# Scaling attention scores in place in PSUM, with their extreme kept as the exponential's bias

## The chip, the core and the metric

The kernel runs on one core of one Trainium2 chip. The metric is the device time of one execution in microseconds (us); lower is better.

## What is computed

A clustered attention feeds two dense layers. There are 2 batches, 8 heads, 768 positions and a head width of 64. A query sees only the keys that have the same nearest centroid (16 centroids per head); where no key has it, every score is the same constant and the softmax is uniform.

```
mask = q_assign[:, :, :, None] == k_assign[:, :, None, :]
scores = scale * np.matmul(q, k.transpose(0, 1, 3, 2))
scores = np.where(mask, scores, -1000000000.0)
scores = scores - np.max(scores, axis=-1, keepdims=True)
attn = np.exp(scores)
attn = attn / (np.sum(attn, axis=-1, keepdims=True) + 1e-09)
x = attn @ v            # then 1536 tokens x 512
h = x @ w_in;  x = (h * sigmoid(h)) @ w_out         # layer 1, 512 -> 2048 -> 512
h = x @ w2_in; y = (max(h,0) + alpha*min(h,0)) @ w2_out   # layer 2, same sizes
```

## The kernel before, in words

**Number format.** All matrix products run on pairs of 16-bit parts (a high and a low half). Before a tensor is split it is brought into range by a power of two (`pow2_scale`, L158); the inverse factors are kept in small columns: `isk` for the keys of a head pair, `q_inv` for the queries of a tile.

**Units.** Attention is cut into 96 units: 12 query tiles of 128 queries (6 for each batch) times 8 heads. Unit u is tile `n = u // 8`, head `h = u % 8`; heads go in 4 pairs that share the prepared keys and values. The function `front` (L449) makes one unit's probabilities:

- TensorE forms 128x768 scores in a two-bank PSUM tile `s` (there are two such tiles), as two halves of 384 columns. For each half one matmul over 80 rows (L459) and one over 128 rows (L463) accumulate. Rows 64 to 79 of the 80-row operands hold the cluster code: the query side is 0 at its own cluster and 2^15 elsewhere, the key side is -2^15 at its own cluster and 0 elsewhere, so that a pair in different clusters gets -2^30.
- VectorE reduces the 768 scores of each query to the negated maximum (L475), then makes in two operations on one column the scale (L478: the product of the inverse factors, or 0 where the maximum shows that no key was in the query's cluster) and the bias (L479: maximum times scale).
- ScalarE computes `exp(scale * score + bias)` from PSUM into SBUF with the row sum as a second output (L481), and copies the result to 16 bits (L488). VectorE subtracts to get the low half (L490). Both go into one of two `hl` buffers.
- A DMA transposes the 128x1536 16-bit block (L496, issued from SyncE's queue, SP). Nothing else issues DMAs, so loads of weights, keys and values stand in that queue too.

`back(u - 2)` multiplies the transposed probabilities of the unit two before by the values (L508, 18 matmuls of 64 columns). After a tile's eighth head `x_done` (L521) normalizes the tile and hands it to layer 1.

**Preparation of keys and queries.** `prep_k_b` (L380) forms the similarities of keys and centroids in the one-bank PSUM tile `m` (one buffer), `one_hot` (L271, L277 to L285) turns them into the cluster code on VectorE, and a DMA transposes the code. It runs once for each of 2 batches and 4 pairs: in batch 0 ahead of unit 0 and after units 0, 2 and 4, in batch 1 after units 44, 46, 48 and 50. `prep_q_b` (L426) does the same for the queries of the next tile, at head 4 of each tile. Sums over partitions (`all_sum`, L207) use the same `m` tile.

**Order of work.** The program text interleaves units with 16 + 16 steps of layer 1 for each of 7 chunks of query tiles (17 units go first; after the chunks 32, 53, 64, 69 and then all 96 units have been issued), and with tasks that convert the weights of layer 1. After the last unit the weights of layer 2 are converted in the background, and layer 2 follows. A planner that runs when the kernel is built then lays out each engine's queue from that text: by priority, and by when its own timing says that operands are ready. On the chip each queue is in order, so an instruction that waits holds back all that stand behind it on that engine.

```
nc.vector.tensor_reduce(out=nm, in_=sc[:, :, :hs], axis=AX.XY, op=ALU.max, negate=True)
nc.vector.tensor_scalar(scl, nm, 2.0 ** 29, d[:, pr:pr + 1], op0=ALU.is_lt, op1=ALU.mult)
nc.vector.tensor_scalar(bias, nm, scl, None, op0=ALU.mult)
```

Of the kernel before, what the change touches and what calls it, by code (L numbers as in the profile page):

```python
# [9 lines left out]
F32 = mybir.dt.float32  # L10
# [36 lines left out]
def cluster_attention_silu_prelu(  # L47
# [44 lines left out]
    def view(off, dt, *dims):  # L92
        n = 1
        for d in dims:
            n *= d
        nb = n * (2 if dt in (F16, BF16) else 4)
        assert off % 4 == 0 and nb % 4 == 0 and off + nb <= total, (off, nb)
        a = arena[:, off // 4:(off + nb) // 4]
        if dt != F32:
            a = a.bitcast(dt)  # L100
        if len(dims) == 1:
            return a
        names = [f"a{i}" for i in range(len(dims))]
        pat = f"p ({' '.join(names)}) -> p {' '.join(names)}"
        return a.rearrange(pat, **{n: d for n, d in zip(names, dims)})
# [39 lines left out]
    def col(n):  # L145
        a = stat[:, nstat[0]:nstat[0] + n]
        nstat[0] += n
        assert nstat[0] <= NSTAT
        return a
# [25 lines left out]
    def scr(n):  # L175
        if scr_pos[0] + n > NSCR:
            scr_pos[0] = 0
        a = scr_cols[:, scr_pos[0]:scr_pos[0] + n]
        scr_pos[0] += n
        return a  # L180
# [55 lines left out]


    half = small_p.tile([128, 12], F32, name="half")

    def prep_centroids():  # L240
        craw = view(o_xf, F32, D)
        nc.sync.dma_start(out=craw, in_=centroids.rearrange("h c d -> (h c) d"))
        nc.vector.memset(ones, 1.0)
        nc.vector.memset(half, 0.5)
        nc.scalar.activation(out=scr(1), in_=half[:, 0:1], func=ACTF.Sqrt)
        make_identity(nc, ident)
        for c in range(C):
            nc.gpsimd.memset(rev[:, c:c + 1], float(C - c))
# [22 lines left out]
    def one_hot(sims, n, w2, o, a, b):  # L271


        y = view(o + KB, F16, n, C)
        z = view(o, F16, n, C)
        m = scr(n)
        nc.vector.reduce_max(out=m, in_=sims, axis=AX.X)  # L277
        nc.vector.tensor_tensor(out=y, in0=sims, in1=bc(m, C), op=ALU.is_equal)
        nc.vector.tensor_tensor(
            out=z, in0=y, in1=rev.unsqueeze(1).to_broadcast([128, n, C]), op=ALU.mult  # L280
        )
        m2 = scr(n // 2).bitcast(F16)
        nc.vector.reduce_max(out=m2, in_=z, axis=AX.X)
        nc.vector.tensor_tensor(out=y, in0=z, in1=bc(m2, C), op=ALU.is_equal)
        nc.vector.tensor_scalar(w2[:, :, D:D + C], y, a, b, op0=ALU.mult, op1=ALU.add)  # L285
# [9 lines left out]
    def k_pre(b, pr):  # L295
        return o_x2 + 6 * KB * pr if b == 0 else o_x2 + (8 + 6 * (pr % 2)) * KB
# [83 lines left out]
    def prep_k_b(b, pr):  # L380
        did.add(("k", b, pr))
        kt1 = view(o_kt1 + 3 * KB * pr, F16, G, 128)
        w2 = view(k_pre(b, pr) + 3 * KB, F16, G, 128)
        sims = psum("m", G, C)
        for g in range(G):
            h = 2 * pr + g // T
            for i, c in enumerate((0, 2)):
                nc.tensor.matmul(
                    out=sims[:, g], lhsT=kt1[:, g], rhs=cw[:, c, h * C:(h + 1) * C],
                    start=(i == 0), stop=(i == 1),  # L390
                )
        one_hot(sims, G, w2, k_pre(b, pr), -MASK, 0.0)
        k_t2[b, pr] = nc.sync.dma_start_transpose(
            out=view(o_kt2 + 3 * KB * pr, F16, G, 128), in_=w2.rearrange("p a b -> p (a b)")
        )


# [28 lines left out]
    def prep_q_b(n):  # L426
        qt1 = view(o_qt + 4 * KB * (n % 2), F16, H, 128)
        w2 = view(o_preq + 2 * KB, F16, H, 128)
        sims = psum("m", H, C)
        for h in range(H):  # L430
            for i in range(2):
                nc.tensor.matmul(
                    out=sims[:, h], lhsT=qt1[:, h], rhs=cw[:, i, h * C:(h + 1) * C],
                    start=(i == 0), stop=(i == 1),
                )
        one_hot(sims, H, w2, o_preq, -MASK, MASK)
        q_t2[n] = nc.sync.dma_start_transpose(
            out=view(o_qt + 4 * KB * (n % 2) + 2 * KB, F16, H, 128),
            in_=w2.rearrange("p a b -> p (a b)"),
        )  # L440


    q_inv = col(2)
    sums = [col(H) for _ in range(2)]
    un_cols = col(24)
    pt_of = {}
    x_ps = {}

    def front(u):  # L449
        n, h = divmod(u, H)  # L450
        b, pr = n // T, h // 2
        sc = ps_s.tile([128, 2, 512], F32, tag="s", name="s")
        qt1 = view(o_qt + 4 * KB * (n % 2), F16, H, 128)
        qt2 = view(o_qt + 4 * KB * (n % 2) + 2 * KB, F16, H, 128)
        kt1 = view(o_kt1 + 3 * KB * pr, F16, 2, T * 128)
        kt2 = view(o_kt2 + 3 * KB * pr, F16, 2, T * 128)
        hs = S // 2
        for j in range(2):
            nc.tensor.matmul(  # L459
                out=sc[:, j, :hs], lhsT=qt2[0:D + C, h],  # L460
                rhs=kt2[0:D + C, h % 2, j * hs:(j + 1) * hs], start=True, stop=False,
            )
            nc.tensor.matmul(  # L463
                out=sc[:, j, :hs], lhsT=qt1[:, h],
                rhs=kt1[:, h % 2, j * hs:(j + 1) * hs], start=False, stop=True,
            )
        d = un_cols[:, 12 + NP * (n % 2):12 + NP * (n % 2) + NP]
        if h == 0:
            nc.vector.tensor_scalar(
                d, isk[b], q_inv[:, n % 2:n % 2 + 1], 1.0 / float(D) ** 0.5,  # L470
                op0=ALU.mult, op1=ALU.mult,
            )
        c0 = 4 * (u % 3)
        nm, scl, bias = (un_cols[:, c0 + i:c0 + i + 1] for i in range(3))
        nc.vector.tensor_reduce(  # L475
            out=nm, in_=sc[:, :, :hs], axis=AX.XY, op=ALU.max, negate=True
        )
        nc.vector.tensor_scalar(scl, nm, 2.0 ** 29, d[:, pr:pr + 1], op0=ALU.is_lt, op1=ALU.mult)  # L478
        nc.vector.tensor_scalar(bias, nm, scl, None, op0=ALU.mult)  # L479
        o = p_buf()  # L480
        nc.scalar.activation(  # L481
            out=view(o, F32, 2, hs), in_=sc[:, :, :hs], func=ACTF.Exp, scale=scl, bias=bias,
            accum_out=sums[n % 2][:, h:h + 1],
        )
        p = view(o, F32, S)
        i = u % 2
        hl = view(o_hl + 3 * KB * i, F16, 2, S)
        nc.scalar.activation(out=hl[:, 0], in_=p, func=ACTF.Copy)  # L488
        en = nc.vector if u in P_LO_DVE else nc.gpsimd
        en.tensor_tensor(out=hl[:, 1], in0=p, in1=hl[:, 0], op=ALU.subtract)  # L490
        pt = view(o_pt + 3 * KB * (u % NPT), F16, 2 * T, 128)
        pt_of[u] = pt
# [584 lines left out]
```

## Time and profile before

| what | value |
|---|---|
| device time, median of 3 runs | 875.75 us (872.88, 875.75, 876.51) |
| profiled execution, first to last instruction (span) | 873.1 us; no device time of its own is given for it |
| busy share of the span: TensorE matmuls / weight loads | 83% / 58% |
| VectorE (DVE) / ScalarE (ACT) / GpSimd (POOL) | 69% / 53% / 13% |
| DMA, mean share of 16 engines | 54.2% |

PE is TensorE's matmuls and PEld its weight loads, which overlap. A row of a group of instructions gives its source line, engine, operation, what it writes and reads, the count, busy us and mean ns of one, and the idle time of the engine just before. A row of waits gives who waited for whom, the total us, how often, and the longest. In the rows of order in time the first two numbers are start and length in us. The span is 2.65 us below the median of the runs.

### The profile page before, as it was taken

The numbers are of one execution on the slowest core, as the hardware profiler recorded it, in microseconds if no ns is written. First come the engines' busy times: TensorE is split into PE (matmuls) and PEld (weight loads), VectorE is DVE, ScalarE is ACT, GpSimd is POOL, SyncE is SP. The second block draws the span as 40 slices with busy tenths as digits, with TensorE's granted clock in tenths as the row PEclk, the third lists the DMA queues.
The fourth block names the chain that finished last, engine by engine and source line by source line (L and its number), as shares of the span: only waits on it lengthen the run. The fifth ranks groups of instructions, "written<-read, shape, count | busy, mean of one in ns | idle before, by whom it ended". The sixth has DMA issues, their size and how long they took to land.

```text
span 873.1 us, 16736 instructions
## 1 busy us (share of the span) xinstructions
PE 721.3 (83%) x6740; PEld 503.3 (58%) x6740; DVE 598.1 (69%) x1366; ACT 459.6 (53%) x825; POOL 109.8 (13%) x89
## 2 busy tenths in 40 slices
PE   2456457668688888899799996899898999999998
PEld 1344346566576776688677786787443444444443
DVE  6899988898978957855975884677995058206700
ACT  7945666747857745745754764868561014102200
POOL 3512200070202210000000001012046000000000
PEclk9965558969999999999999999899998999999999
DMA  9998996767897794763785696227300000000000
GB/s 281 246 258 205 264 205 134 116 121 147 161 171 119 139 164 73 146 116 46 126 121 100 112 212 153 97 98 252 135 1 1 37 12 1 13 25 12 1 25 25
DMA packets 241598, 101.89 MB, mean 117 GB/s; under 512 B 217329, under 2 KB 227569, under 8 KB 241393
## 3 DMA queue, kind: packets, MB, share of 16 engines
q1 hardware_dynamic: 241520, 100.83, 54.2%
q8 instruction: 53, 0.87, 0.4%
q14 instruction: 25, 0.20, 0.1%
HBM read 44.08 MB, written 3.15 MB: 54 GB/s over the span
## 4 chain that ended last, share of the span: by engine, by line
PE 41%; DMA 12%; DVE 9%; ACT 3%; issue 2%; POOL 0%; SPq 0%; POOLq 0%; ACTq 0%; DVEq 0%
PE w L979 10%; DMA arena<-arena 9%; PE w L948 7%; PE w L876 6%; PE m L979 5%; PE w L845 5%; PE m L948 3%; PE x L508 2%; DMA arena<-in_moe_w_in_dram 1%; DMA arena<-in_moe_w_out_dram 1%; DVE stat L475 1%; DVE arena L595 1%; PE s L463 1%; PE s L459 1%; DVE arena L856 1%
## 5 line engine op out<-in xcount | busy, mean ns | idle before, releaser
L845 PE MATMUL w<-arena 128*128 128x256 f16 (+1 forms) x1212 | 132.1, 263 | 14.7 <-DVE arena L852 7.3
L845 PEld LDWEIGHTS <-arena 128*128 128x128 f16 x1344 | 119.3, 101 | 36.3 <-issue 12.9
L508 PE MATMUL x<-arena 128*128 128x64 f16 x1728 | 74.1, 201 | 74.8 <-DMA arena<-arena 74.8
L876 PEld LDWEIGHTS <-arena 128*128 128x128 f16 x1344 | 119.4, 101 | 21.0 <-POOL arena L606 4.0
L876 PE MATMUL w<-arena 128*128 128x256 f16 (+1 forms) x1200 | 124.4, 262 | 6.3 <-POOL arena L606 3.7
L508 PEld LDWEIGHTS <-arena 128*128 128x128 f16 x1728 | 65.2, 103 | 88.7 <-DMA arena<-arena 87.0
L481 ACT ACTIVATE arena<-s,stat 128x768 f32<-128x768 f32 x96 | 94.4, 984 | 41.3 <-DVE stat L479 35.6
L490 DVE TENSOR_TENSOR arena<-arena 128x768 f16<-128x768 f32 x96 | 93.3, 973 | 28.6 <-ACT arena L488 28.1
L475 DVE TENSOR_REDUCE stat<-s 128x1 f32<-128x768 f32 x96 | 91.2, 952 | 29.1 <-PE s L463 28.7
L979 PEld LDWEIGHTS <-arena 128*128 128x128 f16 x576 | 56.8, 99 | 71.8 <-issue 5.1
L948 PEld LDWEIGHTS <-arena 128*128 128x128 f16 x576 | 56.6, 99 | 71.5 <-issue 6.8
L488 ACT ACTIVATE arena<-arena 128x768 f16<-128x768 f32 x96 | 80.5, 840 | 28.3 <-DMA arena<-arena 27.7
L979 PE MATMUL w<-arena 128*128 128x512 f16 x384 | 85.4, 383 | 2.4 <-DVE arena L958 2.4
L948 PE MATMUL w<-arena 128*128 128x512 f16 x384 | 86.4, 379 | 0.8 <-DVE arena L958 0.8
L594 POOL TENSOR_SCALAR arena<-arena,stat 128x1024 f16<-128x1024 f32 x20 | 33.8, 1696 | 401.3 <-DVE stat L168 269.3
L961 ACT ACTIVATE arena<-arena,stat 128x512 f16<-128x512 f32 x48 | 34.3, 720 | 88.5 <-DVE arena L958 88.5
L459 PE MATMUL s<-arena 80*128 80x384 f16 x192 | 69.6, 362 | 5.3 <-DMA arena<-arena 2.7
L463 PE MATMUL s<-arena 128*128 128x384 f16 x192 | 69.9, 364 | 0.0
L573 ACT ACTIVATE arena<-arena 128x1024 int32<-128x1024 uint32 x32 | 36.6, 1145 | 47.9 <-DMA arena<-in_moe_w_in_dram 32.4
L851 ACT ACTIVATE arena<-w,stat 128x256 f32<-128x256 f32 (+1 forms) x101 | 43.8, 434 | 29.2 <-PE w L845 25.4
L957 DVE TENSOR_SCALAR arena<-w,stat 128x512 f32<-128x512 f32 x32 | 23.9, 748 | 46.8 <-PE w L948 46.6
L584 DVE SCALAR_TENSOR_TENSOR arena<-arena 128x1024 int32<-128x1024 int32 x32 | 39.1, 1222 | 24.4 <-ACT arena L577 24.4
(141 smaller groups left out, 1035.4 us busy)
## 6 DMA issues: line engine op xcount, KB each, us to landing
arena<-in_moe_w_in_dram SPq DMA_DIRECT2D x16, 1024.0 KB, 6.0
arena<-in_moe_w_out_dram SPq DMA_DIRECT2D x16, 1024.0 KB, 5.0
arena<-in_k_dram SPq DMA_DIRECT2D x8, 384.0 KB, 4.1
arena<-in_q_dram SPq DMA_DIRECT2D x6, 512.0 KB, 4.5
arena<-in_v_dram SPq DMA_DIRECT2D x8, 384.0 KB, 6.2
out_dram<-arena SPq DMA_DIRECT2D x12, 256.0 KB, 2.0
arena<-arena SPq DMA_TRANSPOSE x149, 4.1
arena<-in_moe_alpha_dram SPq DMA_DIRECT2D x1, 1024.0 KB, 5.1
```

The costliest lines, as they stand in the source:

```text
L459: nc.tensor.matmul(out=sc[:, j, :hs], lhsT=qt2[0:D + C, h], rhs=kt2[0:D + C, h % 2, j * hs:(j + 1) * hs], start=True, stop=False,)
L463: nc.tensor.matmul(out=sc[:, j, :hs], lhsT=qt1[:, h], rhs=kt1[:, h % 2, j * hs:(j + 1) * hs], start=False, stop=True,)
L475: nc.vector.tensor_reduce(out=nm, in_=sc[:, :, :hs], axis=AX.XY, op=ALU.max, negate=True)
L481: nc.scalar.activation(out=view(o, F32, 2, hs), in_=sc[:, :, :hs], func=ACTF.Exp, scale=scl, bias=bias, accum_out=sums[n % 2][:, h:h + 1],)
L488: nc.scalar.activation(out=hl[:, 0], in_=p, func=ACTF.Copy)
L490: en.tensor_tensor(out=hl[:, 1], in0=p, in1=hl[:, 0], op=ALU.subtract)
L508: nc.tensor.matmul(out=x_ps[0][:, h], lhsT=pt[:, ph * T + t], rhs=vt[:, h % 2, t, vh], start=(i == 0), stop=(i == 3 * T - 1),)
L845: nc.tensor.matmul(out=hp, lhsT=wi[:, a, kd, f % 2 * 128:f % 2 * 128 + 128], rhs=mov(bb, kd), start=(i == 0), stop=(i == 3 * KD - 1),)
L851: nc.scalar.activation(out=th, in_=hp, func=ACTF.Tanh, scale=dh[:, f // 2:f // 2 + 1])
L876: nc.tensor.matmul(out=acc, lhsT=wo[:, a, f % 2, dt * 128:(dt + 1) * 128], rhs=g[:, f, bb], start=(i == 0), stop=(i == 3 * KF - 1),)
L948: nc.tensor.matmul(out=hp, lhsT=in_piece(o_a + 24 * KB, f // 2)[:, a, kd, f % 2 * 128:][:, :128], rhs=x[bb][:, kd], start=(i == 0), stop=( ...
L979: nc.tensor.matmul(out=acc, lhsT=g[:, f, a, t * 128:(t + 1) * 128], rhs=out_piece(o_w, f // 2)[:, bb, f % 2], start=(i == 0), stop=(i == 3 ...
```

## The change

The three VectorE operations of a unit become one. `tensor_scalar` multiplies the 768 scores in PSUM by a negative factor per query, writes them back to the same place, and keeps their minimum as a second output; `exp` then takes the scale -1.0 and that minimum as its bias. The factor (`nd_cols`) is made per tile, for all 8 heads together, by the new `head_scales`; in the first tile of a batch it is made pair by pair. The rule "scale 0 where no key is in the query's cluster" moves into that factor: after a pair's keys are coded, 12 one-column matmuls over the code (`missing`) and one comparison set `has` to 1 for each cluster that has a key; 8 one-column matmuls per tile (`own`) then pick the entry for each query's cluster. For this the zero of the code changes sides (key side 2^15 elsewhere and 0 at its own cluster, query side -2^15 at its own and 0 elsewhere); the products are the same.

```diff
@@ -236,12 +236,14 @@
 
 
     half = small_p.tile([128, 12], F32, name="half")
+    has = small_p.tile([128, B, H], F16, name="has")
 
     def prep_centroids():
         craw = view(o_xf, F32, D)
         nc.sync.dma_start(out=craw, in_=centroids.rearrange("h c d -> (h c) d"))
         nc.vector.memset(ones, 1.0)
         nc.vector.memset(half, 0.5)
+        nc.vector.memset(has, 0.0)
         nc.scalar.activation(out=scr(1), in_=half[:, 0:1], func=ACTF.Sqrt)
         make_identity(nc, ident)
         for c in range(C):
@@ -389,9 +391,20 @@
                     out=sims[:, g], lhsT=kt1[:, g], rhs=cw[:, c, h * C:(h + 1) * C],
                     start=(i == 0), stop=(i == 1),
                 )
-        one_hot(sims, G, w2, k_pre(b, pr), -MASK, 0.0)
+        one_hot(sims, G, w2, k_pre(b, pr), -MASK, MASK)
         k_t2[b, pr] = nc.sync.dma_start_transpose(
             out=view(o_kt2 + 3 * KB * pr, F16, G, 128), in_=w2.rearrange("p a b -> p (a b)")
+        )
+        missing = psum("m", 2)
+        for j in range(2):
+            for t in range(T):
+                nc.tensor.matmul(
+                    out=missing[0:D + C, j:j + 1], lhsT=w2[:, j * T + t, 0:D + C],
+                    rhs=rev[:, C - 1:C], start=(t == 0), stop=(t == T - 1),
+                )
+        nc.vector.tensor_scalar(
+            has[D:D + C, b, 2 * pr:2 * pr + 2], missing[D:D + C], MASK * (S - 0.5), None,
+            op0=ALU.is_lt,
         )
 
 
@@ -433,16 +446,41 @@
                     out=sims[:, h], lhsT=qt1[:, h], rhs=cw[:, i, h * C:(h + 1) * C],
                     start=(i == 0), stop=(i == 1),
                 )
-        one_hot(sims, H, w2, o_preq, -MASK, MASK)
+        one_hot(sims, H, w2, o_preq, -MASK, 0.0)
         q_t2[n] = nc.sync.dma_start_transpose(
             out=view(o_qt + 4 * KB * (n % 2) + 2 * KB, F16, H, 128),
             in_=w2.rearrange("p a b -> p (a b)"),
         )
 
+    def head_scales(n, pairs):
+
+        b = n // T
+        qt2 = view(o_qt + 4 * KB * (n % 2) + 2 * KB, F16, H, 128)
+        d = d_cols[:, NP * (n % 2):NP * (n % 2) + NP]
+        if pairs[0] == 0:
+            nc.vector.tensor_scalar(
+                d, isk[b], q_inv[:, n % 2:n % 2 + 1], 1.0 / float(D) ** 0.5 / MASK,
+                op0=ALU.mult, op1=ALU.mult,
+            )
+        h0, nh = 2 * pairs[0], 2 * len(pairs)
+        own = psum("m", nh)
+        for i in range(nh):
+            nc.tensor.matmul(
+                out=own[:, i:i + 1], lhsT=qt2[0:D + C, h0 + i], rhs=has[0:D + C, b, h0 + i:h0 + i + 1],
+                start=True, stop=True,
+            )
+        o = H * (n % 2) + h0
+        nc.vector.tensor_tensor(
+            out=nd_cols[:, o:o + nh].rearrange("p (a b) -> p a b", b=2),
+            in0=own.rearrange("p (a b) -> p a b", b=2),
+            in1=bc(d[:, pairs[0]:pairs[0] + len(pairs)], 2), op=ALU.mult,
+        )
+
 
     q_inv = col(2)
     sums = [col(H) for _ in range(2)]
-    un_cols = col(24)
+    d_cols, nd_cols = col(2 * NP), col(2 * H)
+    un_cols = col(3)
     pt_of = {}
     x_ps = {}
 
@@ -464,22 +502,19 @@
                 out=sc[:, j, :hs], lhsT=qt1[:, h],
                 rhs=kt1[:, h % 2, j * hs:(j + 1) * hs], start=False, stop=True,
             )
-        d = un_cols[:, 12 + NP * (n % 2):12 + NP * (n % 2) + NP]
-        if h == 0:
-            nc.vector.tensor_scalar(
-                d, isk[b], q_inv[:, n % 2:n % 2 + 1], 1.0 / float(D) ** 0.5,
-                op0=ALU.mult, op1=ALU.mult,
-            )
-        c0 = 4 * (u % 3)
-        nm, scl, bias = (un_cols[:, c0 + i:c0 + i + 1] for i in range(3))
-        nc.vector.tensor_reduce(
-            out=nm, in_=sc[:, :, :hs], axis=AX.XY, op=ALU.max, negate=True
-        )
-        nc.vector.tensor_scalar(scl, nm, 2.0 ** 29, d[:, pr:pr + 1], op0=ALU.is_lt, op1=ALU.mult)
-        nc.vector.tensor_scalar(bias, nm, scl, None, op0=ALU.mult)
+        if n % T == 0:
+            if h % 2 == 0:
+                head_scales(n, [pr])
+        elif h == 0:
+            head_scales(n, list(range(NP)))
+        bias = un_cols[:, u % 3:u % 3 + 1]
+        nc.vector.tensor_scalar(
+            sc[:, :, :hs], sc[:, :, :hs], nd_cols[:, H * (n % 2) + h:H * (n % 2) + h + 1], None,
+            op0=ALU.mult, op1=ALU.min, accum_out=bias,
+        )
         o = p_buf()
         nc.scalar.activation(
-            out=view(o, F32, 2, hs), in_=sc[:, :, :hs], func=ACTF.Exp, scale=scl, bias=bias,
+            out=view(o, F32, 2, hs), in_=sc[:, :, :hs], func=ACTF.Exp, scale=-1.0, bias=bias,
             accum_out=sums[n % 2][:, h:h + 1],
         )
         p = view(o, F32, S)
```

## Rows read from the trace of the kernel before

**Rows 1.** Stages: busy us (count) of PE, PEld, DVE, ACT, POOL; clock; DMA share; GB/s.

```profile
25.00:135.00 110.00, 58.31 (x576) 43.24 (x577) 99.28 (x238) 70.91 (x96) 22.93 (x15) 0.65 0.99 232
135.00:200.00 65.00, 46.90 (x694) 40.01 (x692) 57.41 (x135) 40.72 (x88) 18.82 (x10) 0.88 0.70 127
200.00:265.00 65.00, 51.40 (x878) 43.52 (x877) 52.88 (x140) 46.77 (x102) 5.93 (x4) 1.00 0.89 155
265.00:330.00 65.00, 55.42 (x656) 45.98 (x655) 52.05 (x145) 40.50 (x82) 13.91 (x10) 0.97 0.79 136
330.00:535.00 205.00, 186.45 (x2150) 155.56 (x2148) 146.10 (x360) 125.49 (x249) 0.00 (x0) 0.98 0.68 122
...
660.00:873.00 213.00, 209.26 (x967) 94.94 (x965) 75.54 (x110) 35.14 (x51) 9.67 (x4) 0.99 0.04 15
```

**Rows 2.** Groups by line and shape, whole span: VectorE's three operations.

```profile
L475 DVE TENSOR_REDUCE stat<-s 128x1 f32<-128x768 f32 x96 | 91.2, 952 | 29.1 <-PE s L463 28.7
...
L478 DVE TENSOR_SCALAR stat<-stat 128x1 f32<-128x1 f32 x96 | 19.6, 207 | 0.3
L479 DVE TENSOR_SCALAR stat<-stat 128x1 f32<-128x1 f32 x96 | 19.6, 208 | 0.6
```

**Rows 3.** One stretch, L475 alone: stretch, length, busy us (count), clock, DMA.

```profile
25.00:265.00 240.00, 45.11 (x48) 0.81 0.88 183
```

**Rows 4.** Order in time, 213 to 223 us: one unit's front, and VectorE's queue.

```profile
213.59 0.33 PE L459 MATMUL s<-arena 80*128 80x384 f16 x1
...
213.76 0.33 PE L463 MATMUL s<-arena 128*128 128x384 f16 x1
...
214.46 0.96 DVE L475 TENSOR_REDUCE stat<-s 128x1 f32<-128x768 f32 x1 [0.71 <-PE s L463]
215.33 0.95 DVE L490 TENSOR_TENSOR arena<-arena 128x768 f16<-128x768 f32 x1
...
216.92 0.21 DVE L478 TENSOR_SCALAR stat<-stat 128x1 f32<-128x1 f32 x1
...
217.04 0.28 DVE L852 SCALAR_TENSOR_TENSOR arena<-arena,w 128x128 f32<-128x128 f32 x1
...
219.87 0.21 DVE L479 TENSOR_SCALAR stat<-stat 128x1 f32<-128x1 f32 x1
...
220.49 0.98 ACT L481 ACTIVATE arena<-s,stat 128x768 f32<-128x768 f32 x1
...
222.24 0.33 PE L459 MATMUL s<-arena 80*128 80x384 f16 x1
```

**Rows 5.** Waits of the whole span; the last row is 330 to 535 us alone.

```profile
PE x L508 <- DMA arena<-arena: 74.8, 55, 7.8
ACT arena L481 <- DVE stat L479: 35.6, 24, 4.7
ACT arena L488 <- DMA arena<-arena: 27.7, 23, 4.2
...
ACT arena L481 <- DVE stat L479: 25.1, 13, 4.7
```

**Rows 6.** Groups by line and shape: the nearest rows for the new VectorE operations.

```profile
L957 DVE TENSOR_SCALAR arena<-w,stat 128x512 f32<-128x512 f32 x32 | 23.9, 748 | 46.8 <-PE w L948 46.6
...
L277 DVE TENSOR_REDUCE stat<-m 128x8 f32<-128x128 f32 x12 | 3.4, 285 | 1.9 <-PE m L432 1.9
L161 DVE TENSOR_SCALAR stat<-m 128x1 int32<-128x1 int32 x22 | 3.3, 150 | 6.7 <-PE m L212 6.7
...
L620 DVE DVE_READ_ACCUMULATOR arena<-s,arena 128x1 f32 x16 | 1.3, 84 | 0.0
```

**Rows 7.** Order in time on PE, 207 to 212 us: two groups of small matmuls.

```profile
207.27 0.55 PE L432 MATMUL m<-arena 128*128 128x16 f16 x16
...
211.70 0.33 PE L212 MATMUL m<-stat,arena 128*128 128x1 f32 x2
```

**Rows 8.** PE's longest wait for a reader of the one `m` tile.

```profile
PE m L388 <- DVE arena L278: 3.3, 1, 3.3
```

## The prediction

> **What bounds the kernel now.** First the stages. Between 25 and 265 us VectorE is the fullest engine, 99.3 of 110, 57.4 of 65 and 52.9 of 65 us, while PE is at 53%, 72% and 79% [rows 1]. From 330 to 535 us it is PE, 186.5 of 205, with VectorE at 71%. After 660 us PE is busy 98% of the time and no unit is left, so that stretch can only move as a whole. The gain has to come before 535 us: in the first part from VectorE's queue, in the second from the 18.5 us in which PE stands idle.
>
> Second, a unit's three operations: 952, 207 and 208 ns [rows 2], 96 times. Third, their places in the queue. In the unit that starts at 213.59 us the reduction begins at 214.46, L478 only at 216.92, L479 at 219.87 and `exp` at 220.49 [rows 4]: 5.6 us from the start of the reduction to the end of the bias, for operations of 1.37 us in sum. Other VectorE work stands between them, because the planner fills the gap that each dependence leaves. The PSUM tile stays taken meanwhile: `exp` ends at 221.47, and the unit two later writes its scores at 222.24.
>
> Fourth, the waits. ScalarE waits 35.6 us for L479, 25.1 of them between 330 and 535 us, which leaves 10.5 before [rows 5]. PE waits 74.8 us for transposed probabilities, the far end of the same chain.
>
> **VectorE's share.** The new operation has no row of its own: it reads 128x768 in PSUM with a factor per query, writes PSUM and has a second output. The nearest is L957, 748 ns for 512 columns from PSUM with a factor per partition, but into SBUF [rows 6]. Reductions from PSUM take 285 ns for 128 columns and 952 for 768 [rows 6, 2], 1.04 ns a column, so L957 at 768 columns would be 748 + 256 x 1.04 = 1015 ns. The second output is an instruction of its own, 84 ns at L620 [rows 6]; together 1.10 us against 1.37. Bounds: 0.95 us if it costs no more than the reduction; 1.015 + 0.80 + 0.08 = 1.90 us if reading and writing one bank took two steps of 1.04 ns for each column. I take 1.10, since L957 is nearest in kind.
>
> In the queue the rows overlap. L475 at 214.46 is followed at 215.33, L478 at 216.92 at 217.04 [rows 4]: slots of 0.87 and 0.12 us, and with L479 taken like L478 a unit takes 1.11 us of the queue. The new pair, with the same 0.09 off, takes 0.93 to 1.01 us, middle 0.97, and saves 0.14 us. 48 units lie between 25 and 265 us [rows 3]: 6.7 us less.
>
> The Trainium skill (VectorE: DVE Perf Modes, section "The DRAIN you can't avoid") says that the next operation does not start until the pipeline is empty. By that, durations would count in full, 0.27 us a unit, 12.9 us here, and the sum below would end at 858. The trace has L852 starting 0.09 us before L478's row ends, so I keep slots.
>
> Added on VectorE: 8 comparisons (`has`), 18 products (one for each of ten tiles, four for each first tile) and a memset, all of a few columns. Between 0.12 (a slot) and 0.21 us (L478's row), near L161's 150 ns from PSUM [rows 6]: I take 0.16. Fourteen of them lie before 265 us, 2.2 us. The product of the inverse factors once a tile only changes its constant. Net there: 6.7 - 2.2 = **4.5 us less**.
>
> **The chain's share.** The two hand-overs go; what stood between them does not, and will stand before or behind the new operation. So I don't count the 5.6 us. Of ScalarE's 10.5 us of waiting for L479 before 265 us I take half, **5.2 us less**: the next limit is close, since ScalarE's copy to 16 bits already waits 27.7 us for the transpose that frees its buffer [rows 5], and nothing in that loop is shortened. Of the 25.1 us after 330 us I take a quarter, **6.3 us less**, because PE has only 18.5 us of idle time there. The bounds for each are nothing and the whole wait.
>
> **PE's share.** 96 `own` and 96 `missing` matmuls of one column. Sixteen of 16 columns take 0.55 us, 0.034 each; two of one column on 32-bit weights 0.33 us, 0.165 each [rows 7]. The new ones have 16-bit weights like the first: 0.035, 6.7 us in all. Half lies where VectorE is fuller and PE idles, and is free while that holds; the half after 257 us stands in PE's way, **3.4 us more** (upper end 15.8). `missing` needs the coded keys and the single `m` tile; PE's queue is in order, so the scores and layer 1's matmuls stand behind it. PE's longest wait of that kind is 3.3 us [rows 8]; I take **1 us more** in all. No DMA is added or moved; the transposes keep their size, and SP's queue its order as far as the text goes. The swapped sides of the code and the constant scale of `exp` change immediates only and cost nothing, with no cover needed.
>
> **Sum:** -4.5 - 5.2 - 6.3 + 3.4 + 1.0 = -11.6 us. The working stands on the profiled span, 873.1 us, which would become 861.5; what lies around it, 2.65 us to the median, is kept: 875.75 - 11.6 = **864 us**.
>
> **Rivals.** *Nothing to measure.* The freed time is taken by the next loop (copy, low half, transpose, buffer free again), whose waits are in the trace [rows 5], and by PE after 330 us. Then only VectorE's 4.5 us is left against 4.4 us added: 875 us. For it: the DMA engines are 89% to 99% busy in two of the three early stages [rows 1]. Against it: in the unit shown it was L479 that `exp` waited for.
>
> *The chain was the limit.* If the number of units in flight is what sets the pace, cutting about 2.3 us of a chain near 15 us (15%) gives 0.15 x 130 = 20 us between 135 and 265 us, and with some 10 us of PE's idle time after 330 us, 845 us. For it: the scores at 222.24 follow the `exp` that frees their tile by 0.8 us. Against it: VectorE has only 10% to 19% of idle time there.
>
> *In-place PSUM at two steps a column*, slower. Place: VectorE's queue between 25 and 265 us. At 1.90 us the slots go from 1.11 to about 1.82, 48 x 0.71 = 34 us more, with 2.2 + 4.4 us of additions and 5 us of hand-overs still saved: about 911 us. It decides once the operation's row passes about 1.3 us. Against it: accumulating matmuls read and write a bank too, and L463 starts 0.17 us after L459 for the same 384 columns as a plain write [rows 4]. The Trainium skill (PSUM — Partial Sum Buffer, section "PSUM bank collisions raise a hardware error") calls each bank of a partition a separate RAM and bars two engines from it in one cycle; of one instruction that reads and writes it says nothing, and read strictly it would give this case's time. No run here shows it.
>
> *PE waiting at `missing`*, slower. Place: 257 to 330 us, where the keys of batch 1 are coded and PE is busy 55.4 of 65 us [rows 1]. Four `missing` and four pairwise `own` groups take the `m` tile in turn, each behind VectorE. At 2.5 us each the 1 us above becomes 20: 883 us. It turns the sign once the mean passes 1.6 us (12.6 / 8). Against it: the transposed code needed by the same units takes a DMA more, so there is time.
>
> **Chances.** Forecast (854 to 871) 0.50; chain 0.17; nothing 0.20; `missing` 0.08; two steps 0.05. A difference of 0.5%, 4.4 us, is about what a measurement of this kernel can tell from no change. Faster is the first two, 0.67; same 0.20; slower 0.13. The range reaches to the chain's 845 with a margin of 2, and to just short of the wait at `missing`: 843 to 882 us; outside are the two-step case and the ends of the chain and wait cases, nearly 2 in 10.
>
> **What would show it.** Right: the scaling row near 1.02 us with an accumulator read near 0.08 behind it; no VectorE work between it and `exp` but the queue's; ScalarE's 35.6 us of waiting on the bias cut by half or more; PE's wait for transposes below 74.8 us; VectorE about 10 us less busy. Wrong: a row above 1.3 us; PE waits of some us at `missing` or `own`; or the same end of attention near 535 us with the waits moved to the `hl` buffers. The forecast would also fail if the planner, given one operation for three, lays the queues out so that PE meets its waits elsewhere; no row of before can price that.

## Result, and the profile after

The changed kernel takes 868.21 us (median of 6 runs, 864.36 to 872.70) against 876.13 us for the kernel before (6 runs): a ratio of 0.9915, 95% interval 0.989 to 0.9941. A second measurement, on the chip of the first experiments, gave 865.25 us against 875.61 (ratio 0.9882, 0.985 to 0.9915). So the change is worth 8 to 10 us; 864 was forecast. The profiled execution spans 866.6 us, 6.5 less than before.

The head of the page of the changed kernel: busy us, share of the span and instructions of each engine.

```profile
span 866.6 us, 17064 instructions
...
PE 727.8 (84%) x6932; PEld 513.1 (59%) x6932; DVE 587.7 (68%) x1297; ACT 451.9 (52%) x825; POOL 108.5 (13%) x89
```

VectorE is 10.4 us less busy (598.1 us before), ScalarE 7.7 us less (459.6), PE 6.5 us more (721.3).

The groups by line and shape of the changed kernel. L511 is the scaling operation with its accumulator read, L516 `exp`, L523 the copy to 16 bits, L543 the product with the values, L401 `missing`, L468 `own`.

```profile
L516 ACT ACTIVATE arena<-s,stat 128x768 f32<-128x768 f32 x96 | 85.8, 894 | 43.8 <-DVE s L511 34.7 <-DVE arena L525 6.1 <-PE m L212 1.5
...
L511 DVE TENSOR_SCALAR_CACHE_REDUCE s<-s,stat 128x768 f32<-128x768 f32 x96 | 97.2, 1022 | 14.2 <-PE s L501 13.8
...
L523 ACT ACTIVATE arena<-arena 128x768 f16<-128x768 f32 x96 | 80.3, 843 | 50.0 <-DMA arena<-arena 49.4
L543 PE MATMUL x<-arena 128*128 128x64 f16 x1728 | 75.2, 202 | 49.9 <-DMA arena<-arena 49.9
...
L511 DVE DVE_READ_ACCUMULATOR s<-s,stat 128x1 f32 x96 | 13.7, 143 | 0.0
...
L401 PE MATMUL m<-rev,arena 128*80 128x1 f16 x96 | 6.5, 195 | 5.8 <-DVE arena L287 5.8
...
L468 PE MATMUL m<-has,arena 80*128 80x1 f16 x96 | 5.1, 166 | 1.6 <-DVE arena L280 1.3 <-DVE has L405 0.2
```

Set beside [rows 2] and [rows 5]: one operation of 1022 ns and its read of 143 ns stand for three. `exp` waits for VectorE 34.7 us, hardly less than the 35.6 before. PE's wait for transposed probabilities fell from 74.8 to 49.9 us, and ScalarE's wait for the transpose that frees its `hl` buffer rose from 27.7 to 49.4 us. `missing` (L401) made PE wait 5.8 us; it and `own` (L468) keep PE busy for 11.6 us.

The order in time on VectorE, changed kernel:

```profile
343.70 1.02 DVE L511 TENSOR_SCALAR_CACHE_REDUCE s<-s,stat 128x768 f32<-128x768 f32 x1
344.63 0.14 DVE L511 DVE_READ_ACCUMULATOR s<-s,stat 128x1 f32 x1
344.63 0.42 DVE L891 SCALAR_TENSOR_TENSOR arena<-arena 128x256 f16<-128x256 f32 x1
```

The next operation starts with the accumulator read, so the pair takes 0.93 us of the queue, where three operations took 1.11 [rows 4].

The stages (busy us of PE, PEld, DVE, ACT, POOL, clock, DMA share, GB/s), to be read beside [rows 1]; the last row is the first three together:

```profile
25.00:135.00 110.00, 63.95 (x666) 49.15 (x666) 99.09 (x235) 69.64 (x104) 23.04 (x15) 0.92 0.89 223
135.00:200.00 65.00, 50.40 (x735) 42.52 (x732) 55.22 (x117) 39.16 (x87) 19.14 (x10) 0.87 0.71 131
200.00:265.00 65.00, 48.54 (x816) 40.88 (x815) 48.82 (x131) 45.65 (x98) 6.52 (x5) 0.97 0.96 161
265.00:330.00 65.00, 58.81 (x717) 50.00 (x716) 47.62 (x137) 39.08 (x82) 13.64 (x10) 0.97 0.67 123
330.00:535.00 205.00, 181.95 (x2146) 150.75 (x2145) 150.84 (x341) 131.09 (x268) 3.29 (x2) 0.97 0.73 135
...
25.00:265.00 240.00, 162.89 (x2211) 132.54 (x2211) 203.12 (x481) 154.44 (x287) 48.70 (x30) 0.92 0.86 181
```

VectorE is as full between 25 and 135 us as before (99.1 us, 99.3 before); between 135 and 330 us it is busy 151.7 us in place of 162.3 (sums of three rows each).

**Where the time came from, and where it stayed.** Four marks are enough: unit 48 (the first of batch 1) at its product with the values, the last unit at the same point, the last layer-1 matmul, and the end. First unit 48, in order of time on PE, before and after:

```profile
307.12 0.70 PE L508 MATMUL x<-arena 128*128 128x64 f16 x18 [0.53 <-DMA arena<-arena]
```

```profile
306.25 0.60 PE L543 MATMUL x<-arena 128*128 128x64 f16 x15
```

Then the instructions of one line, with duration min/median/max and the first and last start; the kernel before (values, layer 1's second product):

```profile
L508 PE MATMUL x<-arena x1728: 189/193/261, 47.8 to 533.4; 128*128 128x64 f16 x192
...
L876 PE MATMUL m<-arena x144: 269/273/273, 524.1 to 601.1; 128*128 128x256 f16 x144
```

and the changed one:

```profile
L543 PE MATMUL x<-arena x1728: 189/193/261, 47.3 to 510.9; 128*128 128x64 f16 x192
...
L911 PE MATMUL m<-arena x144: 269/273/273, 534.3 to 599.3; 128*128 128x256 f16 x144
```

At unit 48 the change has gained 0.9 us. At the end of attention it has gained 22.5 us, at the end of layer 1 only 1.8, and at the end 6.5. A second profile of the changed kernel (the first run below) has 0.6, 26.1, 6.4 and 11.0 us at the same marks, so the last two differ by some 5 us from one execution to another; the course is the same. Neither half of that was forecast in this form, and the experiments ask why.

### The profile page after: what moved, and what is told of

Read it like the earlier page. It is cut to its first block, busy times and chain, and to the rows that moved or that the text cites. A ratio compares the mean times of both kernels' runs of the same rounds, so it can differ in the third digit from the quotient of the medians.

```text
span 866.6 us, 17064 instructions
## 1 busy us (share of the span) xinstructions
PE 727.8 (84%) x6932; PEld 513.1 (59%) x6932; DVE 587.7 (68%) x1297; ACT 451.9 (52%) x825; POOL 108.5 (13%) x89
## 4 chain that ended last, share of the span: by engine, by line
PE 44%; DMA 22%; DVE 19%; ACT 7%; issue 4%; POOL 2%; SPq 1%; ACTq 0%; POOLq 0%; DVEq 0%
DMA arena<-arena 16%; PE w L1014 10%; PE w L911 7%; PE w L983 6%; PE w L880 6%; PE m L1014 5%; DMA arena<-in_moe_w_in_dram 4%; PE m L983 4%; PE x L543 3%; DVE s L511 2%; DVE arena L630 2%; DMA arena<-in_moe_w_out_dram 2%; DVE arena L525 2%; DVE arena L997 2%; DVE arena L619 2%
## 5 line engine op out<-in xcount | busy, mean ns | idle before, releaser
L911 PEld LDWEIGHTS <-arena 128*128 128x128 f16 x1344 | 118.0, 100 | 21.6 <-POOL arena L641 4.8
L543 PE MATMUL x<-arena 128*128 128x64 f16 x1728 | 75.2, 202 | 49.9 <-DMA arena<-arena 49.9
L516 ACT ACTIVATE arena<-s,stat 128x768 f32<-128x768 f32 x96 | 85.8, 894 | 43.8 <-DVE s L511 34.7
L511 DVE TENSOR_SCALAR_CACHE_REDUCE s<-s,stat 128x768 f32<-128x768 f32 x96 | 97.2, 1022 | 14.2 <-PE s L501 13.8
L523 ACT ACTIVATE arena<-arena 128x768 f16<-128x768 f32 x96 | 80.3, 843 | 50.0 <-DMA arena<-arena 49.4
L543 PEld LDWEIGHTS <-arena 128*128 128x128 f16 x1728 | 66.9, 104 | 64.1 <-DMA arena<-arena 61.3
L996 ACT ACTIVATE arena<-arena,stat 128x512 f16<-128x512 f32 x48 | 34.6, 721 | 91.1 <-DVE arena L993 89.1
L501 PE MATMUL s<-arena 128*128 128x384 f16 x192 | 70.4, 367 | 0.0
```

Of the source, the lines that this page charges most:

```text
L501: nc.tensor.matmul(out=sc[:, j, :hs], lhsT=qt1[:, h], rhs=kt1[:, h % 2, j * hs:(j + 1) * hs], start=False, stop=True,)
L511: nc.vector.tensor_scalar(sc[:, :, :hs], sc[:, :, :hs], nd_cols[:, H * (n % 2) + h:H * (n % 2) + h + 1], None, op0=ALU.mult, op1=ALU.min, ...
L516: nc.scalar.activation(out=view(o, F32, 2, hs), in_=sc[:, :, :hs], func=ACTF.Exp, scale=-1.0, bias=bias, accum_out=sums[n % 2][:, h:h + 1],)
L543: nc.tensor.matmul(out=x_ps[0][:, h], lhsT=pt[:, ph * T + t], rhs=vt[:, h % 2, t, vh], start=(i == 0), stop=(i == 3 * T - 1),)
L911: nc.tensor.matmul(out=acc, lhsT=wo[:, a, f % 2, dt * 128:(dt + 1) * 128], rhs=g[:, f, bb], start=(i == 0), stop=(i == 3 * KF - 1),)
```

## Experiments

Every run was timed beside the kernel before on its own chip. Its medians there were 875.61 us for the first four runs, 874.27 for the next four, 874.94 for the last four.

**The changed kernel again**, no edit.

> The changed kernel once more, beside the three others on the same chip. Both theories: about 868 us, 7 to 9 us below the kernel before.

865.25 us, ratio 0.9882 (0.985 to 0.9915); its span of 862.1 us is the base for the three that follow.

**The hand-overs put back.** After the scaling operation (`un_cols` gets six more columns to hold the results):

```diff
+        for i in (1, 2):
+            b2 = un_cols[:, 3 * i + u % 3:3 * i + u % 3 + 1]
+            nc.vector.tensor_scalar(b2, bias, ones[:, 0:1], None, op0=ALU.mult)
+            bias = b2
```

> The changed kernel with two column operations put back between the scaling operation's minimum and the exponential, so that the bias again goes through three VectorE operations; nothing else differs. Theory (the gain comes from VectorE's queue and from the two hand-overs): 2 x 0.12 us of the queue come back 96 times, and the wait from the scaling to the bias returns to 3 us or more; the gain is lost and the added matmuls stay, 876 to 882 us. Rival (the gain comes from the exponential, whose row fell from 984 to 894 ns): the exponential keeps its 894 ns, so 868 to 871 us.

892.52 us, ratio 1.0191 (1.0159 to 1.0223). `exp` still took 0.9 us, so the rival falls: two operations on one column cost 27 us, although each takes 0.12 us of the queue (the median from the start of L517 below to the next start). From the start of the big VectorE operation to the start of `exp` the mean over the 96 units is 4.63 us before, 2.74 us after, 4.59 us here. What the planner puts between them is seen in VectorE's order in time:

```profile
359.44 1.02 DVE L511 TENSOR_SCALAR_CACHE_REDUCE s<-s,stat 128x768 f32<-128x768 f32 x1 [1.13 <-PE s L501]
360.39 0.14 DVE L511 DVE_READ_ACCUMULATOR s<-s,stat 128x1 f32 x1
360.39 0.17 DVE L567 TENSOR_SCALAR stat<-stat 128x8 f32<-128x8 f32 x1
360.46 0.74 DVE L430 SCALAR_TENSOR_TENSOR arena<-arena,stat 128x512 f16<-128x512 f32 x1
361.12 0.28 DVE L437 COPY arena<-arena 128x512 f16<-128x512 f16 x1
361.33 0.41 DVE L891 SCALAR_TENSOR_TENSOR arena<-arena,w 128x256 f32<-128x256 f32 x1
361.66 0.20 DVE L517 TENSOR_SCALAR stat<-stat,arena 128x1 f32<-128x1 f32 x1
```

Four operations come between the accumulator read and the first of the two column operations. But the theory had 876 to 882 us, and the run is 10 us beyond that; the last experiment but one takes this up.

**`exp` with its scale from a column.**

```diff
+    minus = small_p.tile([128, 1], F32, name="minus")
...
+        nc.vector.memset(minus, -1.0)
...
-            out=view(o, F32, 2, hs), in_=sc[:, :, :hs], func=ACTF.Exp, scale=-1.0, bias=bias,
+            out=view(o, F32, 2, hs), in_=sc[:, :, :hs], func=ACTF.Exp, scale=minus, bias=bias,
```

> The changed kernel with the exponential's scale -1.0 read from a column instead of given as a constant; nothing else differs. Both theories: the exponential's row goes back from 894 towards 984 ns. Theory (hand-overs and queue): ScalarE is busy 52% of the span, so at most 2 us are lost, 868 to 870 us. Rival (the exponential's 90 ns): 96 x 0.09 = 8.6 us of ScalarE are back and the gain with them, 874 to 877 us.

869.78 us, ratio 0.9941 (0.9917 to 0.9965), 4.5 us above the changed kernel beside it, where the theory allowed 2. The group of `exp` in this run:

```profile
L518 ACT ACTIVATE arena<-s,stat,minus 128x768 f32<-128x768 f32 x96 | 94.3, 983 | 35.7 <-DVE s L513 25.7 <-DVE arena L527 4.9 <-PE x L545 3.9
```

The row is back at 983 ns, against 894. The result lies between the two theories: the constant scale is worth some 4.5 of the 10.4 us, the rest comes without it. The size is not firm: set against the first measurement of the changed kernel (ratio 0.9915) it is 2.3 us.

**Without the per-head factors.** `missing`, `has`, `own` and the products (called the additions from here on) are gone, the factor comes from the pair, and the case of a query whose cluster has no key is left out:

```diff
...
-            sc[:, :, :hs], sc[:, :, :hs], nd_cols[:, H * (n % 2) + h:H * (n % 2) + h + 1], None,
+            sc[:, :, :hs], sc[:, :, :hs], d_cols[:, NP * (n % 2) + pr:NP * (n % 2) + pr + 1], None,
```

> The changed kernel without the per-head factors: no counting matmuls, no comparison, no picking matmuls and no products; each query's factor is the pair's. It leaves out the case of a query whose cluster has no key. Theory (the additions cost PE and the m tile what was forecast): 3.4 + 1.0 us on PE and about 2 us on VectorE are saved, 861 to 864 us. Rival (PE's idle time hides the additions): within 2 us of the changed kernel, 866 to 870 us.

865.54 us against 865.25: no difference in the time, as the rival has it. But the additions are not free inside the kernel. First the kernel before: the similarities of the fourth pair's keys on PE, and the first VectorE operation of unit 6, the first unit that uses this pair:

```profile
40.04 0.79 PE L388 MATMUL m<-arena 128*128 128x16 f16 x24 [3.34 <-DVE arena L278]
...
71.07 0.95 DVE L475 TENSOR_REDUCE stat<-s 128x1 f32<-128x768 f32 x1
```

The changed kernel, with `missing` (L401) and `own` (L468) of the third pair ahead of the same similarities (L390), and the product (L473) ahead of unit 6:

```profile
62.67 0.94 PE L401 MATMUL m<-rev,arena 128*80 128x1 f16 x12
...
63.86 0.19 PE L468 MATMUL m<-has,arena 80*128 80x1 f16 x2 [0.25 <-DVE has L405]
64.30 0.79 PE L390 MATMUL m<-arena 128*128 128x16 f16 x24 [0.25 <-DVE stat L473]
...
88.80 0.16 DVE L473 TENSOR_TENSOR stat<-m,stat 128x2 f32<-128x2 f32 x1
...
89.07 1.02 DVE L511 TENSOR_SCALAR_CACHE_REDUCE s<-s,stat 128x768 f32<-128x768 f32 x1
```

And this run, with unit 48 at its values in the last line:

```profile
40.19 0.79 PE L388 MATMUL m<-arena 128*128 128x16 f16 x24 [3.78 <-DVE arena L278]
...
65.21 1.02 DVE L482 TENSOR_SCALAR_CACHE_REDUCE s<-s,stat 128x768 f32<-128x768 f32 x1
...
286.32 0.83 PE L514 MATMUL x<-arena 128*128 128x64 f16 x18 [0.64 <-DMA arena<-arena]
```

The similarities, `missing` and `own` take the one `m` tile in turn, and each group waits until VectorE has read the one before. With the additions the fourth pair's similarities come 24 us later, and unit 6 begins 18 us later than before the change; without them it begins 6 us earlier than before, and unit 48 comes 20.8 us earlier. So an early gain was there to be had with the transposes as they are, and in the changed kernel the additions set the first units back. The earlier units are worth nothing at the end: layer 1's last matmul starts at 606.4 us in this run, 7 us later than in the changed kernel. By 265 us 707 of layer 1's 2688 matmuls had started here, and 798 in the changed kernel: as units ran ahead, layer 1 fell behind. An earlier unit does not make an earlier end.

**Less PE work**, before and after. In both multiplications of layer 1:

```diff
-                for a, bb in ((0, 0), (0, 1), (1, 0)):
+                for a, bb in ((0, 0), (0, 1)):
...
```

> The kernel before with one of three products left out in each of layer 1's two multiplications (the low half of the weights is not used there), a third of layer 1's matmuls and some 80 us of PE. It is the base for the next run. Expected about 800 us by both theories.

> The changed kernel with the same products of layer 1 left out. In the profile of the changed kernel the last unit ends 22.5 us earlier, but layer 1 only 2 us earlier. Theory (PE's queue is full of layer 1 work after attention, so units that end earlier only hand the time to layer 1): with a third of that work gone the time shows, and this run is 15 to 25 us below the run before it. Rival (the end hangs on the conversion of layer 2's weights, whatever PE does): 5 to 11 us below it, as with all products.

864.78 us (ratio 0.9887, 0.9847 to 0.9927) and 838.97 us (0.9595, 0.9563 to 0.9626): with a third of layer 1's matmuls gone the change is worth 25.8 us, just above the theory's 15 to 25. The base surprised: some 800 us were expected, and the kernel before gained only 9.5 us from losing them. Its lines for the values, for layer 1's second product and for the conversion of layer 2's weights, in the run with less PE work:

```profile
L508 PE MATMUL x<-arena x1728: 189/193/261, 48.1 to 523.7; 128*128 128x64 f16 x192
...
L876 PE MATMUL m<-arena x96: 269/273/418, 505.7 to 577.7; 128*128 128x256 f16 x96
...
L618 PE MATMUL s<-arena x128: 218/294/311, 508.3 to 633.1; 128*128 128x128 bf16 x128
```

Layer 1 ends 23 us earlier than in the full kernel before (577.7, 601.1). Attention ends only 10 us earlier (523.7, 533.4), the conversion, which starts while the last unit is under way (508.3 here), only 4 us (633.1, 637.3), and the end comes 10 us earlier (863.0, 873.1). So before the change the time did not follow PE's work, though PE was 91% busy beside the units: the units' chain held attention, and through the conversion the end. The values' line of the changed kernel with less PE work:

```profile
L543 PE MATMUL x<-arena x1728: 189/193/261, 47.0 to 493.6; 128*128 128x64 f16 x192
```

Here attention ends 30 us earlier than in the run before it, and the end comes 25.8 us earlier. In the full kernels the two limits stood close together; the change shortened the chain, and PE's queue was left in front.

**More units earlier, and a faster conversion.** Two settings of the changed kernel:

```diff
-UNITS_BY_CHUNK = (32, 53, 64, 69, 98, 98, 98)
+UNITS_BY_CHUNK = (32, 53, 64, 78, 98, 98, 98)
```

> The changed kernel with nine more units issued during chunk 3 of layer 1 (78 in place of 69), so that attention ends earlier and the conversion of layer 2's weights starts earlier; layer 1's work is the same. Theory (PE is full until layer 1 ends, and layer 2's first part waits for converted weights): layer 1 ends within 3 us of where it did, layer 2 takes 5 to 12 us less from its start to the end, 856 to 863 us. Rival (the conversion is hidden by then): within 3 us of the changed kernel.

```diff
-W2_TASKS = 1
+W2_TASKS = 2
```

> The changed kernel with two tasks of layer 2's weight conversion issued for each step of layer 1 after attention in place of one. Theory (layer 2's first part waits for converted weights): layer 2 takes 5 to 12 us less from its start to the end; layer 1 may end up to 5 us later, as VectorE and ScalarE serve both; 858 to 866 us in all. Rival (the conversion is held by its loads and its own chain, not by where it stands in the text): within 3 us of the changed kernel.

867.15 us (ratio 0.9927, 0.99 to 0.9953) and 867.66 us (0.9916, 0.9889 to 0.9943): both as the changed kernel. In the first the marks move, and cancel:

```profile
L543 PE MATMUL x<-arena x1728: 189/193/261, 47.7 to 495.8; 128*128 128x64 f16 x192
...
L911 PE MATMUL m<-arena x144: 269/273/273, 534.1 to 604.4; 128*128 128x256 f16 x144
```

Attention ends 15 us earlier than in the changed kernel and layer 1 ends 5 us later. From there to the end it takes 259 us (863.6 - 604.4) in place of 267 (866.6 - 599.3), since layer 2's weights are converted sooner: the last product of that conversion starts at 602.2 us here and at 615.9 in the changed kernel. The sum stays. The half of the theory about the conversion holds, the half about layer 1's end (within 3 us) does not. The second setting moved both marks 3 us later; its rival holds.

**Half of the transpose**, before and after: only the high halves of the probabilities are transposed and used.

```diff
...
-        nc.sync.dma_start_transpose(out=pt_of[u], in_=hl)
+        nc.sync.dma_start_transpose(out=pt_of[u][:, 0:T], in_=hl)
...
-            for ph, vh in ((0, 0), (0, 1), (1, 0)):
+            for ph, vh in ((0, 0), (0, 1)):
...
```

> The kernel before with only the high halves of the probabilities transposed and used (768 columns a unit in place of 1536, 12 matmuls with the values in place of 18); the low halves are still made and not used. It shortens the loop copy, low half, transpose, buffer free. It is the base for the next run. Both theories: some 20 us of PE and half of the transposes' DMA time are gone; 845 to 865 us.

> The changed kernel with the same products left out. In the full kernels unit 48 multiplies its values at 307.1 us before the change and 306.3 after it: no gain in the first half, though the stretch from the scaling to the exponential fell by 2 us. Theory (there the freed time went into the wait for transposes, the loop that frees the hl buffers): with that loop shorter, unit 48 comes 8 us or more earlier than in the run before it. Rival (VectorE's queue, as full before as after, sets the pace there): within 3 us of the run before it.

868.80 us (ratio 0.9927, 0.9894 to 0.996; 845 to 865 were expected) and 840.66 us (0.9599, 0.9571 to 0.9627): 28.1 us between them. The edit also takes a third of the product with the values off PE, so the total does not tell the transposes from PE's work. Unit 48 on PE, the kernel before and then the changed one, both with half of the transpose:

```profile
304.01 0.52 PE L508 MATMUL x<-arena 128*128 128x64 f16 x12 [0.76 <-DMA arena<-arena]
```

```profile
294.83 0.28 PE L543 MATMUL x<-arena 128*128 128x64 f16 x4
```

9.2 us earlier where it was 0.9, as the theory had it. But 7.5 of the 9.2 us are there at unit 16 already (149.5 and 142.0 us at its values). From unit 16 to unit 48 it takes 154.5 and 152.8 us, against 159.3 and 157.8 in the full kernels: the edit gives about 5 us to both, and the change gains 1.7 us there in place of 1.5. What the shorter loop seems to speed up is the catching up after the additions: from unit 6 to unit 16 (the starts of the big VectorE operation) the changed kernel takes 51 us, and 43.5 with half of the transpose; the kernel before takes 64 and 66. So the loop alone does not explain the missing early gain. ScalarE's wait for it in the second of these runs:

```profile
ACT arena L523 <- DMA arena<-arena: 9.7, 9, 2.2
```

It is 9.7 us, against 49.4 in the full changed kernel. In the full kernels the means of units 2 to 47 show where a unit then waits: from the big VectorE operation to `exp` 5.37 us before and 3.20 after, but from `exp` to the copy 2.23 and 3.42, and a unit's whole chain 18.3 and 17.9 us. These means do not set the pace either: without the per-head factors ScalarE waits 48.3 us for the `hl` buffers and a unit's chain is 18.7 us, and units come 20 us earlier.

**The hand-overs put back, without the per-head factors**: the edits of two runs above together.

> The changed kernel with the two column operations put back as in the run handover, and without the per-head factors (it leaves out the case of a query whose cluster has no key). That run took 892.5 us, 17 us more than the kernel before, where the theory had 876 to 882. If the added matmuls and products cost time once the chain is long again: 874 to 880 us. Rival (the in-place operation with its accumulator read is itself dearer than the reduction in such a queue, or the queues are laid out worse): 885 us or more.

899.84 us, ratio 1.0267 (1.021 to 1.0324): 34 us more than without the hand-overs (865.54). The added matmuls are not what made that run slow. This one again has three VectorE operations in a chain, as the kernel before has; the reduction is exchanged for the scaling with its accumulator read, and `exp` is 0.09 us shorter. It is 25 us slower than the kernel before. Its mean from the big operation to `exp` is 5.00 us, against 4.63. That is in the right direction; whether it is the operation, or queues that the planner lays out worse, no run here tells apart, and it stays open. The runs together show what the hand-overs and the additions do early (us; starts of the big VectorE operation of units 6 and 16, and unit 48 at its values):

| kernel | unit 6 | unit 16 | unit 48 | time |
|---|---|---|---|---|
| before | 71.1 | 134.9 | 307.1 | 875 |
| changed: additions, no hand-overs | 89.1 | 140.1 | 306.3 | 868.21, 865.25 |
| additions and hand-overs | 87.6 | 139.1 | 320.9 | 892.52 |
| no additions, no hand-overs | 65.2 | 118.0 | 286.3 | 865.54 |
| no additions, hand-overs | 70.4 | 135.5 | 321.7 | 899.84 |

With the additions unit 16 comes at 139 to 140 us whether the hand-overs are there or not. Without them the hand-overs are worth 17 us at unit 16 and 35 us at unit 48.

**Half of the first 48 low parts on GpSimd.**

```diff
-P_LO_DVE = range(96)
+P_LO_DVE = [u for u in range(96) if u % 2 or u >= 48]
```

> The changed kernel with the low half of every second unit among the first 48 made on GpSimd in place of VectorE; all is computed. VectorE loses 24 x 0.87 us of its queue, GpSimd, busy a fifth of that time, takes 24 x 1.7 us. Theory (VectorE's queue still bounds the first half): unit 48 comes 8 us or more earlier and the whole takes 855 to 863 us. Rival (the first half is bound by transposes and loads, or PE's work takes back what it gains): within 4 us of the changed kernel.

871.97 us, ratio 0.995 (0.9924 to 0.9977): no gain, some 4 to 7 us above the changed kernel. Between 25 and 265 us VectorE has 5 us less to do than in the changed kernel and GpSimd 37 more:

```profile
25.00:265.00 240.00, 166.87 (x2184) 133.95 (x2185) 197.73 (x458) 154.03 (x287) 85.77 (x53) 0.89 0.88 181
```

and unit 48 comes at the same time:

```profile
306.37 0.70 PE L543 MATMUL x<-arena 128*128 128x64 f16 x18 [0.62 <-DMA arena<-arena]
```

The theory falls. The test is not clean, as an operation on GpSimd is longer too (from the start of the low half to the landing the mean of units 2 to 47 is 6.50 us, 5.89 in the changed kernel), and as other work filled VectorE again; what it shows is that taking low parts off VectorE brought nothing. No version that computes all of it beats the changed kernel.

## Why the prediction was right, and which steps were not

The total was right: 864 us forecast, 868.2 and 865.3 measured, in the range and faster. Its steps fared differently, and errors of both signs nearly cancelled; that the total came so close is in part luck.

**The price of the new operation: right.** 1015 + 84 ns were forecast from L957 and L620, 1022 + 143 ns measured. In the queue the pair takes 0.93 us, the lower end of what was given, as the read costs no slot. The next operation starts 0.09 us before the end of L511's row, so durations do not count in full. The Trainium skill (VectorE: DVE Perf Modes, section "The DRAIN you can't avoid") says that the next operation does not start until the pipeline is empty, but also that one that is not held starts earlier; the prediction worked out 858 us from the first half alone, and these rows do not bear that out. VectorE was 10.4 us less busy in all (9.3 by the forecast's own terms: 96 x 0.14 - 26 x 0.16), 6.5 of them between 25 and 265 us (209.6 to 203.1), where 4.5 were forecast.

**The early gain, 4.5 + 5.2 us: the step that failed.** VectorE did lose that work, and unit 48 came 0.9 us earlier. "Between 25 and 265 us VectorE is the fullest engine" was true and did not make its work the measure: with 24 low parts on GpSimd unit 48 came no earlier. The chain's part was there, and larger than forecast: without the additions unit 48 came 20.8 us earlier than before the change, 16.2 of them by unit 16. In the changed kernel the additions, which the text gave 1 us of waiting, set unit 6 back by 18 us first. The loop of copy, low half and transpose, which the text named as "the next limit is close" and let cost half, then seems to limit how fast that is caught up: halving the transpose made 0.9 us at unit 48 into 9.2, 7.5 of them by unit 16. How the loss divides between the two is not shown.

**The late gain, 6.3 us: too small for attention, and the reading of the limit was wrong.** Attention's last unit ended 22.5 us earlier (26.1 in the second profile). The text took PE as the limit from 330 us on because it is 91% busy. In the kernel before it was not in front: a third less of layer 1's matmuls saved 9.5 us there. It came to the front through the change: the same cut then saved 26 to 29 us (838.97 against 865.25 and 868.21, measured on other chips). That is how 22.5 us became 1.8 at the end of layer 1, and 26.1 became 6.4 in the second profile. The 4.7 us that the profile still gains after that (601.1 to the end of 873.1 is 272.0 us, 599.3 to 866.6 is 267.3) go with the conversion of layer 2's weights, which follows attention and whose last product starts at 615.9 in place of 637.3 us.

**PE's share, 3.4 + 1 us: not at the end, and in another place.** Without the additions the kernel takes the same time. Their matmuls kept PE busy for 11.6 us (6.5 + 5.1), where 6.7 were forecast, and `missing` made PE wait 5.8 us, in two waits, one of 4.8. The text looked for their cost among PE's waits and after 257 us. It came in the first tile, as units that start later behind the one `m` tile; the half that "lies where VectorE is fuller and PE idles, and is free" was not free there.

**The constant scale of `exp`: the text had it at nothing.** It took 90 ns from each `exp` and was worth some 2 to 5 us.

**The rivals.** *Two steps a column* fell: the row is 1.02 us, far from 1.82. *PE waiting at `missing`* fell for the time, and its place was wrong; its mechanism, `missing` and `own` taking the `m` tile in turn behind VectorE, is what set the first units back. *Nothing to measure* fell as a whole; its loop of the transposes took a part of the early gain. *The chain was the limit* was nearest to what the runs show: the kernel before was held by the units' chain. Its 20 us between 135 and 265 us did not come; without the additions 20.8 us came at unit 48, most of them before 135 us. Its late part was 22.5 us at the end of attention, of which PE kept most. With PE's work cut, or PE's work and the transposes together, the change is worth 26 to 28 us, where this rival forecast 31.

Of the signs named in advance, the row, VectorE's busy time and PE's shorter wait for transposes came as written; the read took 0.14 us in place of 0.08. One sign of being wrong came too, some us of PE's waiting at `missing`. ScalarE's wait on the bias did not fall by half (34.7 us); with shorter work before it the engine only waits elsewhere, so that this sum was no measure of the gain.

## What to carry to other kernels

A dependence between two tiny operations costs what an ordered queue puts between them, here some 2 us for two operations of 0.12 us each: count the steps from one engine's hand-over to the next, not their durations. An engine that is 90% busy need not be the limit, and one that was not can become it by the change; take work away from it in both versions, and see in which the time moves. Where two limits stand close, a shortened chain pays only up to the next one, so price the loops beside it (buffers, transposes, the work that starts when this stage ends) before counting the whole of it. And look at what an addition stands in front of, not only at how long it takes: here 11.6 us of small matmuls on a shared buffer set back by 18 us the units behind them.

## What was not expected of the hardware

- `exp` over 768 columns took 894 ns with a constant scale and 983 ns with a scale read from a column, the bias coming from a column in both.
- A VectorE operation that reads and writes the same PSUM columns and keeps a minimum took about as long as one that writes SBUF would: 1022 ns for 768 columns, where 1015 was estimated from L957's row.
- Two operations on one column in a unit's chain cost 27 us in 865 (34 without the per-head factors), 0.28 us a unit, for some 0.24 us of VectorE's queue, though moving 0.87 us of that queue's work from every second early unit to GpSimd gained nothing.
